# A batch's mixing units over twelve slots instead of ten, with six feed-forward units held back instead of four

## The chip, the cores and the metric

The kernel runs on one core of one Trainium2 chip. The metric is the device time of one execution in microseconds. The engines are named as in the profile: PE (TensorE matmuls), PEld (TensorE weight loads), DVE (VectorE), ACT (ScalarE), POOL (GpSimd) and SP (SyncE, which issues most of the DMAs here).

## What is computed

For 8 batches of 576 positions: causal attention with a decay (8 heads of 64), then a block that mixes along the positions with a rank of 32 and a feed-forward network of width 2048, with a residual. Cut to what matters:

```python
scores = scale * q @ k.T + (cum[:, None] - cum[None, :])      # causal, cum = cumsum(log f)
x = softmax(scores) @ v                                       # heads side by side: (8, 576, 512)
h = x.T @ U @ V                                               # mixing along the positions
u = x + h.T
out = u + relu(u @ w_ch1) @ w_ch2
```

## The kernel before

**Two sweeps.** The first does all of attention, the mixing, and the part of the feed-forward network that belongs to 6 of the 16 blocks of the hidden width. The second, behind it, does the other 10 blocks. The change is in the first.

**Steps and slots.** Attention goes by pairs of heads: 32 pairs, four to a batch. `step(t)` (line 808) is a software pipeline over them: in step t the pair t is scored, the pair t-1 is turned and multiplied with its values, the pair t-2 is finished. Steps 0 to 31 score; 32 and 33 only finish. Each step has 10 slots (`SLOTS`, line 761), which are numbered 0 to 9 here. In every slot PE gets a few short pieces of attention: a score block `S` or `St` (lines 354 to 358), transposes of the exponentials `T` (453, 467), the values `V` in slots 0 and 7 (528, 556), and some more (`Ty`, `Tx`, `Tt`). Behind them a slot can hold a mixing unit and a filler.

**Who follows a score.** DVE takes the row maximum from the score's bank (378, 404), ACT the exponential (386, 414), which frees the bank. Scores have two PSUM banks (`psS`, line 108; up to pair 5 they borrow from `psF` too), so a score waits for the exponential of the score two before it.

**Mixing units.** When the last pair of batch b has been finished (line 907, at the end of slot 9 of the step before `MIX[b]`), `mix_units(b)` gives ten units: five `H` (`hmix`, line 650: one matmul of 128x512, after which DVE adds it to x, line 651), four `Tu` (line 664: four transposes, then ACT copies them to `uh`, line 654, and DVE writes the remainder `ul`, line 655, two slots later) and one `Tv` (line 673). `MIX` is step 6 for batch 0, then 10, 14, up to 30; the last batch's mixing comes after step 33, in a loop of its own (line 954).

**Feed-forward units, the fillers.** `ffn_units(b)` gives 24 units, 27 for odd b: `A` (`l1`, line 713: 12 matmuls of 128x256 or 128x384; ACT takes the relu into `hh`, line 721, and DVE the remainder `hl`, line 717) and `B` (`l2`, line 731: 6 matmuls of 128x512 into an accumulator that three units share, after which DVE adds x and writes `ost`, line 745). They are placed by `credit` (lines 897 to 903) over the slots of `ROOM` (all but 0 and 7), so that `HELD` of them are left when the next batch's mixing starts; those are run in the mixing slots. A batch's own fillers become available when its mixing is over (line 910).

**Banks.** `H`, `Tu`, `Tv`, `A` and `B` share the pool `psF` of two PSUM banks (line 107). While a `B` accumulator is open over its three units, the others have one bank between them.

**Order.** PE's order is as written in `step`. DVE, ACT and POOL are ordered by a scheduler from the order in which `defer` (line 266) hands their work over.

**After step 33** the loop at line 954 interleaves the last batch's mixing and fillers with the loading and splitting of the second sweep's weights (`wb_unit`, line 939), one unit of each to a pass; the splitting runs on DVE and ACT. This stretch is called the drain here.

Of the kernel before, what the change touches and what calls it, by code (L numbers as in the profile page):

```python
# [40 lines left out]
def tile_decay_attention_moe(ctx, tc, qk, v, f, U, V, w1, w2, out):  # L41
# [219 lines left out]
    filler = []  # L261
# [12 lines left out]
    def run_filler():  # L274
        w, fn = filler.pop(0)
        fn()
        return w
# [482 lines left out]
    NP = B * NHP  # L760
    SLOTS = 10
    ENGINES = (nc.scalar, nc.scalar, nc.gpsimd, nc.gpsimd, nc.gpsimd)
    HELD = 4
    with tc.manual_schedule(engines=None):
        fr, fl, cm0, dq = decay_log()
        nc.sync.dma_start(fr, f)
# [39 lines left out]
    MIX = [SEQ.index(NHP * b + NHP - 1) + 3 for b in range(B)]  # L806

    def step(t):
# [3 lines left out]
        last, ending = t == LAST, t > LAST - 2  # L812
# [7 lines left out]
        for s in range(6 + 2 if last else SLOTS):  # L820
# [69 lines left out]
                ranks(c)  # L890

            if mixing:
                for _ in range(2 if t == MIX[0] else 1):
                    mixing.pop(0)[1]()
                if filler and (s in (0, 1, 3, 5) or ending):
                    run_filler()
            elif len(filler) > HELD and s in ROOM:

                ahead = sum(x >= s for x in ROOM) + len(ROOM) * (min(m for m in MIX if m > t) - 1 - t)
                credit[0] += (len(filler) - HELD) / max(ahead, 1)  # L900
                if credit[0] > 0.999 or t > LAST - 3:
                    credit[0] = max(credit[0] - 1, 0)
                    run_filler()
            if ps_ and s == 6:
                score(p, 1, 0)
            if px and s == (6 + 1 if last else 9) and st[c]["hp"] == NHP - 1:
                b = st[c]["b"]
                assert len(filler) <= HELD and not mixing
                mixing.extend(mix_units(b))
# [9 lines left out]
    with tc.manual_schedule(engines={ET.PE, ET.SP}):  # L919
        step(0)  # L920
    with tc.manual_schedule(engines={ET.PE}):
        for t in range(1, 7):
            step(t)
    with tc.manual_schedule(engines={ET.PE, ET.SP}):
        for t in range(7, LAST + 1):
            step(t)
        run_later()
# [584 lines left out]
```

## Time and profile before

| | us |
|---|---|
| three runs | 1223.8, 1224.58, 1919.21 |
| their median | 1224.58 |
| the profiled execution's own time | 1222.74 |
| its span in the trace | 1221.0 |
| step 6, the mixing of batch 0 | 25.01 |
| step 10, the mixing of batch 1 | 20.69 |
| step 30, the mixing of batch 6 | 20.75 |
| start of step 0, of step 6 and of step 32 | 10.7, 95.8, 670.7 |

The third run of the three stands far from the others and is not used. A step's start is that of its first score on PE. A row of a timeline begins with the start and the duration in us; a number in brackets behind it is how long the engine had been idle and for what. Matmul rows overlap, since the array is pipelined: how long one takes is the distance to the start of the next, not its duration. A row of the windows has the stretch, its length, and then each engine's busy time with its instructions in brackets.

### The profile page before, as it was taken

How to read it: one execution, taken by the hardware profiler on the slowest of the kernel's cores; microseconds unless marked ns; L12 is line 12 of the kernel's file. 1: busy time of each engine (PE TensorE's matmuls, PEld its weight loads, DVE VectorE, ACT ScalarE, POOL GpSimd, SP SyncE). 2: the span in 40 equal slices, each digit the busy share in tenths (PEclk: the TensorE clock that was granted, in tenths of full speed). 3: DMA queues.
4: the chain of work that ended last, by engine and by line, in shares of the span. 5: the costliest groups of instructions: out<-in, count | busy, mean ns of one | idle time of the engine just before them, and what ended most of it. 6: DMA issues, size and time to landing. Idle time of an engine off the chain costs nothing.

```text
span 1221.0 us, 23840 instructions
## 1 busy us (share of the span) xinstructions
PE 1187.8 (97%) x8460; PEld 1084.5 (89%) x8460; DVE 930.3 (76%) x2229; ACT 739.1 (61%) x2027; POOL 541.0 (44%) x538
## 2 busy tenths in 40 slices
PE   8998999999999999999999999999999999999998
PEld 5887898988889988989989888788899999999998
DVE  8887878768778778787686798875777767777675
ACT  7777787767768768777676443334454544545443
POOL 4214554444545435454442000125785556555553
PEclk9999999999999999999999999999999999999999
DMA  5753335335235325425232347132514254243420
GB/s 150 198 139 121 102 93 165 97 80 167 80 81 167 95 73 153 116 71 175 80 103 75 121 154 225 42 104 85 140 53 139 87 139 122 90 136 92 134 53 35
DMA packets 81159, 138.47 MB, mean 113 GB/s; under 512 B 8752, under 2 KB 45616, under 8 KB 78992
## 3 DMA queue, kind: packets, MB, share of 16 engines
q1 hardware_dynamic: 79824, 128.56, 34.9%
q0 software_dynamic: 1152, 8.39, 3.8%
q8 instruction: 67, 1.10, 0.4%
q14 instruction: 52, 0.43, 0.1%
q10 hardware_dynamic: 64, 0.00, 0.0%
HBM read 101.08 MB, written 35.78 MB: 112 GB/s over the span
## 4 chain that ended last, share of the span: by engine, by line
PE 78%; DVE 10%; ACT 6%; DMA 3%; issue 2%; SPq 0%; POOL 0%; DVEq 0%; ACTq 0%; POOLq 0%
PE N L1155 12%; PE A L713 10%; PE A L1135 9%; PE B L731 8%; PE B L1135 7%; PE V L556 5%; PE T L453 4%; PE V L528 3%; PE S L357 3%; PE S L358 2%; DMA sr<-in_w_dram 2%; PE B L1155 2%; PE S L354 2%; PE O L1027 2%; PE O L1220 2%
## 5 line engine op out<-in xcount | busy, mean ns | idle before, releaser
L386 ACT ACTIVATE P<-S,nm 128x128 f32<-128x128 f32 (+3 forms) x256 | 137.8, 540 | 53.8 <-DVE nm L378 47.0
L378 DVE CUSTOM_DVE_ANT_0 S<-S,mask 128x128 f32<-128x128 f32 (+3 forms) x256 | 125.6, 496 | 53.4 <-PE S L358 46.7
L197 POOL TENSOR_TENSOR hb<-xn,hb 128x256 fp32r<-128x256 f32 x136 | 114.2, 860 | 117.3 <-ACT hb L194 99.8
L322 POOL CAST G<-qk 64x576 fp32r<-64x576 f32 x52 | 34.8, 669 | 248.7 <-PE St L358 148.0
L713 PE MATMUL A<-uh,w1h 128*128 128x256 f32 (+1 forms) x384 | 120.5, 314 | 1.9 <-DVE hl L717 1.9
L713 PE MATMUL A<-ul,w1h 128*128 128x256 f32 (+1 forms) x384 | 113.5, 296 | 0.0
L713 PE MATMUL A<-uh,w1l 128*128 128x256 f32 (+1 forms) x384 | 113.5, 296 | 0.0
L194 ACT CAST hb<-xn 128x256 fp32r<-128x256 f32 x136 | 51.8, 404 | 76.6 <-DVE xn L1141 42.8
L731 PE MATMUL B<-w2h,hh 128*128 128x512 f32 x216 | 90.4, 418 | 2.0 <-DVE ost L745 1.0
L453 PE MATMUL T<-ident,P 128*128 128x128 f32 x544 | 85.5, 272 | 0.0
L731 PE MATMUL B<-w2l,hh 128*128 128x512 f32 x216 | 85.0, 394 | 0.0
L731 PE MATMUL B<-w2h,hl 128*128 128x512 f32 x216 | 84.6, 391 | 0.0
L435 DVE TENSOR_TENSOR PTl<-T,PTh 128x512 fp32r<-128x512 f32 (+1 forms) x156 | 79.0, 525 | 6.7 <-ACT PTh L432 6.4
L1155 PE MATMUL N<-sw,hb 128*128 128x256 f32 x546 | 80.9, 283 | 1.0 <-POOL hb L197 0.9
L335 POOL TENSOR_TENSOR G<-qk,G 64x576 fp32r<-64x576 f32 x52 | 74.5, 1434 | 13.1 <-ACT G L322 5.1
L1155 PE MATMUL N<-b2h,hb 128*128 128x256 f32 x420 | 79.8, 282 | 0.0
L336 POOL TENSOR_TENSOR G<-qk,G 64x576 fp32r<-64x576 f32 x52 | 75.4, 1449 | 4.8 <-ACT G L322 4.7
L713 PEld LDWEIGHTS A<-uh,w1h 128*128 128x128 f32 x384 | 72.8, 190 | 4.3 <-DVE hl L717 4.1
L357 PE MATMUL S<-G 128*128 128x128 f32 x208 | 70.2, 343 | 4.9 <-ACT P L386 3.1
L432 ACT CAST PTh<-T 128x512 fp32r<-128x512 f32 (+1 forms) x156 | 68.4, 470 | 10.0 <-PE T L453 9.5
L1155 PEld LDWEIGHTS N<-sw,hb 128*128 128x128 f32 x546 | 71.8, 190 | 1.8 <-POOL hb L197 1.8
L713 PEld LDWEIGHTS A<-uh,w1l 128*128 128x128 f32 x384 | 73.1, 190 | 0.3
(327 smaller groups left out, 4012.2 us busy)
## 6 DMA issues: line engine op xcount, KB each, us to landing
qk<-in_qk_dram SPq DMA_DIRECT2D x104, 288.0 KB
direct<-ud SPq DMA_DIRECT2D x48, 256.0 KB
sr<-in_w_dram SPq DMA_DIRECT2D x20, 512.0 KB
vr<-in_v_dram SPq DMA_DIRECT2D x32, 256.0 KB
accd<-ost SPq DMA_DIRECT2D x32, 256.0 KB
xn<-accd SPq DMA_DIRECT2D x8, 1024.0 KB
out_dram<-xn SPq DMA_DIRECT2D x32, 256.0 KB
ud<-uh SPq DMA_DIRECT2D x7, 1024.0 KB
```

Source lines behind the costliest of these rows:

```text
L197: leng.tensor_tensor(dl, src, dh.bitcast(F32), op=ALU.subtract)
L335: pin(el.tensor_tensor(g[oth, 2, cols], k[oth], gf[oth, 2, cols], op=ALU.subtract))
L336: pin(em.tensor_tensor(g[own, 1, cols], q[own], gf[own, 0, cols], op=ALU.subtract))
L357: nc.tensor.matmul(ps, G[j][:, 0, c0 : c0 + P], G[j][:, 2, cols], start=first, stop=False)
L378: newest["top"] = nc.vector.tensor_tensor_reduce(ps[:, :w], ps[:, :w], mask[:, 512 - w : 512], scale=-SCALE, scalar=3.0e38, op0=ALU.add, o ...
L386: nc.scalar.activation(pt, ps[:, :w], AF.Exp, bias=z["nm"][:, col : col + 1], scale=-1.0, accum_out=z["sm"][:, col : col + 1])
L435: defer(2, lambda: nc.vector.tensor_tensor(dstl, src, dsth.bitcast(F32), op=ALU.subtract))
L453: nc.tensor.transpose(tp[:, P * x : P * x + P], z["P"][j][i][:, P * c : P * c + P], ident)
L713: nc.tensor.matmul(ps[:, :nt], wt[:, fc, c], ut[:, c, sl], start=m == 0, stop=m == 3 * NDC - 1)
L731: nc.tensor.matmul(ps, ht[:, fc, P * x : P * x + P], wt[:, fc], start=fc == 0 and m == 0, stop=fc == NA - 1 and m == 2,)
L1135: nc.tensor.matmul(ps, a[x][:, c], b[y][:, c], start=start and m == 0, stop=m == 5, skip_group_check=not start)
L1155: nc.tensor.matmul(ps[:, y], a[p_][:, P * y : P * y + P], w[q_], start=start and y == 0 and m == 0, stop=stop and y == 1 and m == 2,)
```

## The change

Three things, all in `step`:

- `HELD` goes from 4 to 6: two more feed-forward units of a batch are still to be run when the next batch's mixing starts, and so fewer are placed in the slots before.
- In a mixing step of batches 1 to 6, slots 4 and 9 (`SKIP`) take no mixing unit, so the ten units go over slots 0, 1, 2, 3, 5, 6, 7, 8 and, in the next step, 0 and 1. Slots 4 and 9 take a filler instead; with the slots 0, 1, 3 and 5, which had one before, that is six.
- Batch 0, in step 6, gets one mixing unit per slot over slots 0 to 9; before it was two per slot over slots 0 to 4. Its fillers are available from the end of slot 9 instead of slot 4.

```diff
     NP = B * NHP
     SLOTS = 10
     ENGINES = (nc.scalar, nc.scalar, nc.gpsimd, nc.gpsimd, nc.gpsimd)
-    HELD = 4
+    HELD = 6
+    SKIP = (4, 9)
     with tc.manual_schedule(engines=None):
         fr, fl, cm0, dq = decay_log()
         nc.sync.dma_start(fr, f)
...
             if mixing:
-                for _ in range(2 if t == MIX[0] else 1):
+                if t == MIX[0] or s not in SKIP:
                     mixing.pop(0)[1]()
-                if filler and (s in (0, 1, 3, 5) or ending):
+                if filler and (s in (0, 1, 3, 5) or s in SKIP or ending):
                     run_filler()
             elif len(filler) > HELD and s in ROOM:
```

The slots of `ROOM` that hold no filler, in the steps between two mixings (slots 0 and 7 never hold one, and a mixing unit in slots 0 and 1 is not counted):

| step | before | now |
|---|---|---|
| 7 | 4, 9 | 1, 5 |
| 8 | 3, 8 | 1, 6 |
| 9 | 3, 8 | 2, 6 |
| 12, 13 | 2; none | 1; 3 |
| 15, 16, 17 | 6; 3; 1, 5 | 6; 2, 6; 2, 6 |
| 20, 21 | 9; none | 2; 3 |
| 23, 24, 25 | 6; 3, 9; 6 | 6; 2, 6; 2, 6 |
| 28, 29 | 5; none | 2; 3 |

No instruction is added or removed; they stand elsewhere. In the names below the first number is the batch or pair, the last one only tells buffers apart.

PE in step 6, from the first mixing unit of batch 0, before:

```order
L650 MATMUL H0_0_1268<-TS0_624,VV_112 128x512
L650 MATMUL H0_1_1270<-TS0_624,VV_112 128x512
L357 MATMUL S6_01_1284<-G0_91 128x256
L358 MATMUL S6_01_1284<-G0_91 128x256
...
L650 MATMUL H0_2_1291<-TS0_624,VV_112 128x512
L650 MATMUL H0_3_1293<-TS0_624,VV_112 128x512
L357 MATMUL S6_02_1301<-G0_91 128x384
L358 MATMUL S6_02_1301<-G0_91 128x384
```

and now:

```order
L650 MATMUL H0_0_1268<-TS0_624,VV_112 128x512
L357 MATMUL S6_01_1281<-G0_91 128x256
L358 MATMUL S6_01_1281<-G0_91 128x256
...
L650 MATMUL H0_1_1288<-TS0_624,VV_112 128x512
L357 MATMUL S6_02_1295<-G0_91 128x384
L358 MATMUL S6_02_1295<-G0_91 128x384
```

Two units that followed each other are now a slot apart, and the last of the ten stands in slot 9.

PE in step 10, the end of the mixing of batch 1, from its second `Tu`, before:

```order
L664 MATMUL Tu1_1_2542<-ident_99,xn1_105 128x128 x4
...
L664 MATMUL Tu1_2_2579<-ident_99,xn1_105 128x128 x4
L357 MATMUL S10_12_2593<-G1_92 128x384
...
L664 MATMUL Tu1_3_2611<-ident_99,xn1_105 128x128 x4
L357 MATMUL S10_13_2633<-G1_92 128x512
L358 MATMUL S10_13_2633<-G1_92 128x512
L673 MATMUL Tv1_2636<-ident_99,xn1_105 128x64 x4
L357 MATMUL S11_00_2657<-G0_91 128x128
```

and now:

```order
L664 MATMUL Tu1_1_2563<-ident_99,xn1_105 128x128 x4
L357 MATMUL S10_12_2577<-G1_92 128x384
...
L664 MATMUL Tu1_2_2595<-ident_99,xn1_105 128x128 x4
L357 MATMUL S10_13_2617<-G1_92 128x512
L358 MATMUL S10_13_2617<-G1_92 128x512
L731 MATMUL B0_256_1_2472<-w2h_109,hh0_256_2091 128x512
...
L357 MATMUL S11_00_2644<-G0_91 128x128
...
L664 MATMUL Tu1_3_2668<-ident_99,xn1_105 128x128 x4
```

The `B` accumulator `B0_256_1`, which before was closed in slot 5, is now opened in slot 4 and closed in slot 9, with `Tu1_0`, `Tu1_1` and `Tu1_2` in slots 6, 7 and 8 inside that stretch; `Tu1_3` and `Tv1` have moved to slots 0 and 1 of step 11.

DVE at the start of step 11, around the remainder of `Tu1_3`, before:

```order
L378 ISA S10_13_2633,nm10_2353<-S10_13_2633,mask_93 128x512
L378 ISA nm10_2353 128x1
L655 TENSOR_TENSOR ul0_1311<-Tu1_3_2611,uh0_1310 128x4x128
L378 ISA S11_00_2657,nm11_2641<-S11_00_2657,mask_93 128x128
L378 ISA nm11_2641 128x1
L655 TENSOR_TENSOR ul0_1311<-Tv1_2636,uh0_1310 128x4x64
```

and now, from the values of that step:

```order
L576 TENSOR_TENSOR xT9_2550<-V9_1_2647,cr9_1_2648 64x576
L378 ISA S11_01_2681,nm11_2626<-S11_01_2681,mask_93 128x256
L378 ISA nm11_2626 128x1
L435 TENSOR_TENSOR PTl10_2661<-T10_00_2663,PTh10_2660 128x512
L378 ISA S11_02_2700,nm11_2626<-S11_02_2700,mask_93 128x384
L378 ISA nm11_2626 128x1
L655 TENSOR_TENSOR ul0_1351<-Tu1_3_2668,uh0_1350 128x4x128
```

The remainder of `Tu1_3` stood ahead of every score of step 11 on DVE; it now stands behind the values `V9_1` and behind the score `S11_02` of slot 2, the slot in which the batch's first `A` unit stands on PE.

## The prediction

> **What bounds the kernel now.** The page first: PE is busy nearly all the time, the others are not.
>
> ```profile
> span 1221.0 us, 23840 instructions
> PE 1187.8 (97%) x8460; PEld 1084.5 (89%) x8460; DVE 930.3 (76%) x2229; ACT 739.1 (61%) x2027; POOL 541.0 (44%) x538
> ```
>
> All the idle time of PE is 1221.0 - 1187.8 = 33 us. The change adds and removes no instruction, so what it can win or lose is waits of PE. Next the windows, cut at the starts of steps: 6, 7, 8 with 9, 10 and 30, and the drain.
>
> ```profile
> core 0: us, PE busy (x) PEld busy (x) DVE busy (x) ACT busy (x) POOL busy (x), PEclk, DMA share, GB/s
> 95.81:120.82 25.01, 21.76 (x170) 18.70 (x168) 17.54 (x50) 16.88 (x49) 8.86 (x8) 1.00 0.37 122
> 120.82:142.86 22.04, 20.90 (x161) 19.03 (x159) 18.19 (x50) 15.99 (x47) 11.74 (x10) 1.00 0.34 86
> 142.86:180.92 38.06, 37.99 (x280) 35.30 (x278) 29.93 (x90) 31.06 (x90) 21.26 (x19) 1.00 0.36 96
> 180.92:201.61 20.69, 20.02 (x136) 17.19 (x134) 17.97 (x48) 15.74 (x45) 9.98 (x9) 1.00 0.37 101
> 617.06:637.81 20.75, 20.09 (x136) 17.21 (x134) 17.75 (x47) 15.04 (x43) 9.53 (x9) 1.00 0.36 101
> 685.00:770.00 85.00, 79.52 (x401) 66.07 (x400) 79.28 (x163) 33.68 (x66) 1.00 (x1) 1.00 0.51 164
> ```
>
> PE idles 3.25 us in step 6, 1.14 in step 7, 0.07 in steps 8 and 9, 0.66 to 0.67 in a later mixing step, 5.5 in the drain. Third, the waits of PE, which name these:
>
> ```profile
> PE S L357 <- ACT P L386: 3.1, 4, 0.9
> PE Tu L664 <- DVE ost L745: 2.1, 6, 0.3
> ...
> PE H L650 <- DVE xn L651: 1.3, 2, 0.8
> PE B L731 <- DVE ost L745: 1.0, 6, 0.2
> PE Tu L664 <- DVE ul L655: 1.0, 1, 1.0
> PE S L357 <- ACT Ptl L414: 1.0, 4, 0.2
> ...
> PE Tv L673 <- DVE ul L655: 0.7, 1, 0.7
> ```
>
> H, Tu and Tv in step 6 wait 3.0 us for the evacuation of a bank; in the six later mixing steps one Tu and one B each wait for a B's evacuation (3.1 us in all). So the mixing waits that the change is near come to about 6 us, half a per cent. A wait costs more than its idle time, because the array runs empty:
>
> ```profile
> 182.60 0.60 PE L453 MATMUL T<-ident,P 128*128 128x128 f32 x4
> 182.95 0.48 PE L650 MATMUL H<-TS,VV 128*128 128x512 f32 x1
> ...
> 194.67 0.60 PE L453 MATMUL T<-ident,P 128*128 128x128 f32 x4
> 195.62 0.66 PE L664 MATMUL Tu<-ident,xn 128*128 128x128 f32 x4 [0.35 <-DVE ost L745]
> 198.36 0.60 PE L664 MATMUL Tu<-ident,xn 128*128 128x128 f32 x4
> 200.02 0.62 PE L664 MATMUL Tu<-ident,xn 128*128 128x128 f32 x4
> 201.25 0.43 PE L673 MATMUL Tv<-ident,xn 64*128 64x64 f32 x4
> ```
>
> Four transposes take 0.35 us to the next start without a wait and 0.95 with one of 0.35: the wait cost 0.6, its idle time and 0.25 more. I count 0.25 for every wait.
>
> **Part one, the first batch.** In step 6 one unit per slot leaves each evacuation a slot of time, as in step 10, where no H waits. Two A units also leave the step for step 7; that moves work and is no gain. What keeps step 6 from gaining all of its idle time is the next wait in line, that of the scores for their banks:
>
> ```profile
> 110.92 1.25 ACT L322 CAST G<-qk 128x576 fp32r<-128x576 f32 x2
> 112.07 0.64 ACT L432 COPY PTh<-T_v 128x256 f32<-128x256 f32 x2
> 112.60 0.51 ACT L414 ACTIVATE Ptl<-St,nm 128x288 f32<-128x288 f32 x1
> 113.00 0.21 ACT L414 ACTIVATION_READ_ACCUMULATOR Ptl<-St,nm 128x1 f32 x1
> 113.09 0.51 ACT L414 ACTIVATE Ptl<-St,nm 128x288 f32<-128x288 f32 x1
> ```
>
> The casts need the tail scores St done; only after them come the exponentials that free the banks for the scores of slots 6 and 7, 2.7 us later (110.92 to 113.60). An A unit stood over that time:
>
> ```profile
> 189.63 1.37 PE B L731 x6
> ...
> 204.90 1.44 PE A L713 x12
> ```
>
> Without its 1.44 PE has transposes and two Tu, four groups at 0.35 to 0.45, some 1.6 us, and waits about 1.1. Step 6: up to 3.25 gained, about 1.6 given back there and in the scores before. Step 7 is less crowded at its start, since slots 0 and 1 have no filler; I let it gain 0.7 of its 1.14. Together -2.4 us, bounds -4.4 (both steps without idle time) and +1 (the scores wait as long as the units did).
>
> **Part two, slots that are left empty.** Batch 0's fillers now start a step later, and two fewer are placed in each batch, so more slots of ROOM hold none. An empty slot has its price where ACT is behind, as in step 17, whose slot 1 is empty:
>
> ```profile
> 335.87 0.64 ACT L575 COPY cr<-V 64x576 f32<-64x576 f32 x1 [1.15 <-PE V L556]
> 336.29 0.49 PE L453 MATMUL T<-ident,P 128*128 128x128 f32 x3
> 336.41 0.72 ACT L194 CAST VS<-vr 128x640 fp32r<-128x640 f32 x1
> 337.16 0.37 ACT L386 ACTIVATE P<-S,nm 128x128 f32<-128x128 f32 x1
> 337.67 0.44 PE L357 MATMUL S<-G 128*128 128x384 f32 x1 [0.89 <-ACT P L386]
> ```
>
> cr, VS and the exponential stand in a row, and the score of slot 2 waits 0.89, so 1.1 us. An empty slot 6 before the empty 7 costs 0.5 (the four waits for Ptl, 0.25 each, and 0.25) to 0.7; an empty slot 2 or 3 from nothing to 0.4. Step 8 now leaves 1 and 6 empty and step 9 leaves 2 and 6: 1.1 + 0.6 and 0.4 + 0.6, less the 0.3 that steps 8 and 9 lose now: +2.3 (bounds 0 and +3.5). In steps 11 to 29 more slots 2 and 6 go empty, but slots that cost much now (1 of step 17, 5 of step 17, the score of slot 8 in steps 13, 21 and 29) are filled or relieved; I take +0.5, bounds -3 and +3.
>
> **Part three, the six later mixing steps.** Removed: the waits of B, Tu and Tv, 0.67 of idle time and three times 0.25, and the wait of a score behind Tv, about 0.3: 1.7 us a step. Added: with B open from slot 4 to slot 9, Tu in slots 6, 7 and 8 have one bank, so each needs the remainder ul of the one before. The one in slot 7 has the values V behind its predecessor, over 2 us of PE, and need not wait. The one in slot 8 has this before it:
>
> ```profile
> 198.61 0.64 ACT L575 COPY cr<-V 64x576 f32<-64x576 f32 x1 [0.23 <-PE V L556]
> 199.28 0.75 DVE L576 TENSOR_TENSOR xT<-V,cr 64x576 f32<-64x576 f32 x1 [0.49 <-ACT cr L575]
> 199.96 0.55 DVE L378 CUSTOM_DVE_ANT_0 S<-S,mask 128x384 f32<-128x384 f32 x1
> 200.43 0.68 DVE L655 TENSOR_TENSOR ul<-Tu,uh 128x512 fp32r<-128x512 f32 x1
> ```
>
> The chain hangs on the end of V, just ahead of the Tu of slot 7 (198.36), and ul ends at 201.11; in the kernel before Tv takes that bank at 201.25. The Tu of slot 8 comes at 200.02. In the new order it needs that same bank, so it waits until 201.25: 1.2 us. Behind it on PE are the score of slot 9 and the closing B.
>
> The second new wait is that of the batch's first A unit, in slot 2 of the next step. It takes the bank of the last Tu, in slot 0, whose ul stands behind V's chain, a score, a remainder of transposes and the score of slot 2 itself. With
>
> ```profile
> L435 DVE TENSOR_TENSOR PTl<-T,PTh 128x512 fp32r<-128x512 f32 (+1 forms) x156 | 79.0, 525 | 6.7 <-ACT PTh L432 6.4
> ```
>
> that is, from the end of V, cr 0.64, xT 0.75, score 0.5, PTl 0.53, score 0.55, ul 0.68, with about 0.1 between engines: 3.8 us. PE has eight short groups of 0.25 to 0.45 there, some 2.5 us. It waits 1.3 (bounds 0.5 and 1.9). Per step 1.2 + 1.3 - 1.7 = +0.8, times six +4.8; bounds -3 (the second wait absent) and +9.
>
> [...]
>
> **Part four, the drain.** Two B units (2 x 1.37 = 2.7) now run among the last batch's mixing instead of before it. DVE is busy 79.28 of 85.00 us there and PE idles 5.5, so the units fill waits: 2.2 of the 2.7 are covered, I estimate, since the waits lie spread (bounds 0 and 2.7). If DVE were not late there, all 2.7 would be on the path.
>
> **The sum.** -2.4 + 2.3 + 0.5 + 4.8 - 2.2 = +3.0 us on the profiled execution's 1222.74: 1225.7. The two runs at 1223.8 and 1224.58 lie 1.45 above that execution on average, so 1227.2 on their scale. That is +0.2%; 2% is about what a measurement of this kernel can tell from no change.
>
> **The rivals.** (a) *The new waits stay out*: the units in one bank find it free. Then a mixing step gains its 1.7: 6 x (0.8 + 1.7) = 15 below the forecast, 1212. For it: the two B waits do go away, and DVE has less to do in slots 5 and 6. Against it: the chain from V does not depend on a backlog. With one of the two waits it is 1220. (b) *Slower: ACT falls behind in the emptier slots.* If each of the 14 slots 1, 2 and 6 that are newly empty in steps 8 to 29 cost 0.85, between step 17's 1.1 and the 0.6 of a slot 6, they come to 11.9 instead of the 2.8 of part two: +9, 1236. It decides once scores wait in most of those steps. For it: step 17. Against it: slots 7 and 8 of step 9 are empty now, and steps 8 and 9 idle 0.07 us together. (c) *The drain hides nothing*: the two units come where DVE is not late, 2.2 more, 1229. (d) *More slack than PE's busy time shows.* If the time without weight loads were slack that better spread units could use, as the windows have it, 6.3 us in step 6 and 3.5 in each of six steps, that is 27 us: 1197. Against it: steps 8 and 9 lack 2.8 us of loads while PE idles 0.07, so that time is the matmuls' own.
>
> [...] The trace shows 89% against 97% and shows the loads idle where PE is not, so the matmul time is what I count by.
>
> **How the numbers follow.** Forecast 0.55 (1221 to 1233, its own bounds), (a) 0.17, (b) 0.20, (c) 0.06, (d) 0.02. The range 1214 to 1236 leaves out (d), the lower part of (a) and the upper end of (b). More than 2% faster needs (d): 0.02. More than 2% slower needs 25 us, 4 in each mixing step, more than twice my bounds: 0.02. Within 2%: 0.96.
>
> **What would show it.** Right: in the waits of PE, "Tu <- DVE ul" and "A <- DVE ul", some six times each and near 1 us; no "Tu <- DVE ost"; steps 10 and 11 together some 0.8 us longer for the same work; step 6 near 20 us. Wrong: no Tu waits in slot 8 (part three), step 6 below 19 us (part one), or "S <- ACT P" over 10 us (rival b).

## The result, and the profile after

The changed kernel takes 1236.88 us (median of 5 runs, 1236.5 to 1238.91), the kernel before 1223.8 in the same round: 1.0121 times as long, 95% interval 1.0109 to 1.0133 (the ratio is an estimate of its own, not the quotient of the two medians, which is 1.0107). That is 13 us slower and 0.9 us beyond the upper end of the predicted range; the forecast, 1227.2, was on the right side and some 10 us short.

The profiled execution of the changed kernel is 2.0 us above its median. The first lines of its page:

```profile
span 1237.1 us, 23871 instructions
PE 1192.1 (96%) x8460; PEld 1089.3 (88%) x8460; DVE 935.9 (76%) x2229; ACT 739.1 (60%) x2027; POOL 539.6 (44%) x538
```

PE now idles 45 us instead of 33 and is busy 4.3 us longer with the same 8460 instructions. The waits of PE after the change:

```profile
PE A L713 <- DVE ul L655: 8.5, 6, 1.4
PE Tu L664 <- DVE ul L655: 7.1, 12, 0.7
PE S L357 <- ACT P L386: 3.8, 6, 0.9
PE A L713 <- DVE hl L717: 2.8, 4, 1.0
PE S L357 <- ACT Ptl L414: 2.4, 7, 0.5
PE O L1028 <- DVE hb L999: 2.0, 1, 2.0
```

The first line is new, and in the second six of the twelve waits were not expected; "Tu <- DVE ost" and "B <- DVE ost" (3.1 us together) are gone. The windows, cut at the starts of the same steps as before (6, 7, 8 with 9, 10) and over the drain:

```profile
95.72:116.83 21.11, 18.70 (x145) 15.66 (x143) 16.28 (x47) 15.33 (x46) 9.11 (x9) 1.00 0.17 46
116.83:139.70 22.87, 21.27 (x174) 19.91 (x172) 19.40 (x55) 17.98 (x52) 12.55 (x12) 1.00 0.57 175
139.70:180.27 40.57, 39.11 (x280) 35.50 (x279) 30.12 (x88) 30.58 (x89) 20.54 (x19) 1.00 0.34 90
180.27:203.16 22.89, 21.70 (x140) 18.99 (x139) 18.84 (x50) 16.53 (x46) 10.19 (x10) 1.00 0.30 80
698.32:784.00 85.68, 79.96 (x402) 66.85 (x403) 78.94 (x163) 34.79 (x67) 1.00 (x1) 1.00 0.53 169
```

Step 6 still idles 2.4 us, steps 8 and 9 now 1.5 instead of 0.07, a mixing step 1.2 instead of 0.7. Since two B units run later, lengths are compared for the same work in this table (1.37 us for each B unit that a stretch has less or more):

| stretch | before | now | difference | of it work | rest | forecast |
|---|---|---|---|---|---|---|
| steps 6 to 9 | 85.11 | 84.55 | -0.56 | -2.7 | +2.2 | -0.1 |
| steps 10 to 29 | 436.14 | 444.84 | +8.70 | 0 | +8.7 | } +5.3 |
| step 30 to the first T of the last pair | 44.46 | 49.08 | +4.62 | +1.4 | +3.2 | } |
| from there to PE's end | 554.07 | 557.55 | +3.48 | +1.4 | +2.1 | -2.2 |

The rest sums to 16.2 us, within 0.1 the difference of the two spans, where the forecast had 3.0. Each difference is one execution against one. Steps 10 and 11 alone, before and now:

```profile
180.92:223.85 42.93, 42.20 (x305) 38.14 (x304) 34.96 (x99) 34.01 (x96) 21.13 (x19) 1.00 0.50 147
```

```profile
180.27:226.35 46.08, 43.41 (x311) 39.49 (x310) 35.58 (x99) 33.86 (x95) 20.58 (x19) 1.00 0.47 137
```

They take 3.15 us more, 1.37 of it for one B unit more: 1.8 us a mixing step, where the prediction had 0.8. Steps 14 and 15, 18 and 19, 22 and 23, 26 and 27 give the same, 1.75 to 1.78 us each, and all other steps from 10 to 29 together -0.1: the whole of the 8.7 lies in the mixing steps and the steps just behind them. Where it goes shows in the order of time. The transposes of slot 7, which "need not wait" (timeline of the changed kernel, start, length, engine):

```profile
196.50 0.68 DVE L435 TENSOR_TENSOR PTl<-T,PTh 128x512 fp32r<-128x512 f32 x1
...
197.10 0.42 DVE L378 CUSTOM_DVE_ANT_0 S<-S,mask 128x256 f32<-128x256 f32 x1
...
197.44 0.68 DVE L655 TENSOR_TENSOR ul<-Tu,uh 128x512 fp32r<-128x512 f32 x1
...
198.27 0.63 PE L664 MATMUL Tu<-ident,xn 128*128 128x128 f32 x4 [0.46 <-DVE ul L655]
```

The remainder of the Tu before them is queued on VectorE behind a remainder of transposes and a score, and ends at 198.12. Later, the Tu of slot 8 and the first A unit:

```profile
200.84 0.63 PE L664 MATMUL Tu<-ident,xn 128*128 128x128 f32 x4 [0.73 <-DVE ul L655]
...
205.09 0.64 ACT L575 COPY cr<-V 64x576 f32<-64x576 f32 x1 [1.18 <-PE V L556]
205.28 0.60 PE L664 MATMUL Tu<-ident,xn 128*128 128x128 f32 x4
...
205.77 0.75 DVE L576 TENSOR_TENSOR xT<-V,cr 64x576 f32<-64x576 f32 x1 [0.99 <-ACT cr L575]
...
206.44 0.41 DVE L378 CUSTOM_DVE_ANT_0 S<-S,mask 128x256 f32<-128x256 f32 x1
...
207.21 0.60 ACT L654 CAST uh<-Tu 128x512 fp32r<-128x512 f32 x1
...
207.35 0.69 DVE L435 TENSOR_TENSOR PTl<-T,PTh 128x512 fp32r<-128x512 f32 x1 [0.39 <-ACT PTh L432]
...
207.96 0.56 DVE L378 CUSTOM_DVE_ANT_0 S<-S,mask 128x384 f32<-128x384 f32 x1
...
208.43 0.69 DVE L655 TENSOR_TENSOR ul<-Tu,uh 128x512 fp32r<-128x512 f32 x1
...
209.26 0.36 PE L713 MATMUL A<-uh,w1h 128*128 128x256 f32 x1 [1.43 <-DVE ul L655]
```

This is the chain that the prediction had worked out: the fourth Tu is done at 205.88, its ul runs 2.6 us later, behind V's evacuation, two scores and a PTl, and A waits 1.43 us for the bank. In the kernel before, that ul is over well ahead of the first A unit, which doesn't wait:

```profile
202.57 0.69 DVE L655 TENSOR_TENSOR ul<-Tu,uh 128x512 fp32r<-128x512 f32 x1
...
204.66 0.36 PE L713 MATMUL A<-uh,w1h 128*128 128x256 f32 x1
```

One more loss had no place in the sum: the granted clock. In the windows of the changed kernel, 3.41 us wide, before and behind the first A unit of the last pair's step and before and behind the wait of O:

```profile
650.91:654.32 3.41, 1.92 (x15) 1.37 (x14) 2.99 (x8) 3.38 (x12) 1.55 (x1) 1.00 0.22 82
654.32:657.73 3.41, 3.41 (x16) 3.11 (x16) 0.98 (x5) 0.83 (x3) 0.00 (x0) 0.50 1.03 374
...
780.61:784.02 3.41, 1.36 (x6) 0.84 (x5) 3.41 (x9) 1.55 (x4) 0.00 (x0) 1.00 0.18 73
784.02:787.43 3.41, 3.41 (x9) 2.63 (x8) 3.41 (x9) 0.41 (x1) 0.00 (x0) 0.50 0.00 0
```

The number behind those of POOL is the clock: 0.50 for 3.41 us, twice, and PE is busy throughout, so up to 1.7 us are lost each time. In the profile of the kernel before no such stretch lies within the work of PE. That is one execution: the mean clock of its others lies between 0.997 and 1.000, so it need not be free of them.

### The profile page after: what moved, and what is told of

Read it like the earlier page. It is cut to its first block, busy times and chain, and to the rows that moved or that the text cites. A ratio compares the mean times of both kernels' runs of the same rounds, so it can differ in the third digit from the quotient of the medians.

```text
span 1237.1 us, 23871 instructions
## 1 busy us (share of the span) xinstructions
PE 1192.1 (96%) x8460; PEld 1089.3 (88%) x8460; DVE 935.9 (76%) x2229; ACT 739.1 (60%) x2027; POOL 539.6 (44%) x538
## 4 chain that ended last, share of the span: by engine, by line
PE 70%; DVE 9%; ACT 7%; DMA 2%; issue 2%; POOL 0%; DVEq 0%; ACTq 0%; POOLq 0%
PE N L1156 11%; PE A L713 9%; PE A L1136 9%; PE B L731 9%; PE B L1136 7%; PE V L556 5%; PE T L453 3%; PE S L357 2%; DMA sr<-in_w_dram 2%; PE S L358 2%; PE O L1221 2%; PE B L1156 2%; PE O L1028 2%; ACT PTh L432 1%; ACT G L322 1%
```

## The experiments

Each ratio is to the kernel before, timed in the same round.

**The first batch alone.** The kernel before with

```diff
-                for _ in range(2 if t == MIX[0] else 1):
+                for _ in range(1):
```

> The kernel before with the first batch's part alone: one mixing unit per slot over slots 0 to 9 of step 6; no empty slots for the later batches, four fillers held. In the trace of the changed kernel step 6 still stands still for 3.9 us, though its mixing units wait for nothing: the scores of slots 2 and 3 (0.93 and 0.77) and the tail scores now wait for the exponentials. Theory (the wait has only changed its place, and the slots that run empty in steps 7 to 9 cost something too): no gain, the start of step 10 about 2 us later once the same work is counted, the whole 1 to 3 us longer than the kernel before, so 1225 to 1227 where before takes 1223.8. Rival (the first batch's part is sound and all of the loss lies in the later batches): 1 to 3 us shorter, 1221 to 1223.

Measured: 1220.6 us, ratio 0.9986 (0.9977 to 0.9995). The rival was right: this part is sound, and the kernel is the only one of the study that beats the kernel before. It is not for the reason that I had, though. Steps 6 to 9 of this kernel:

```profile
96.65:181.64 84.99, 81.12 (x607) 73.20 (x605) 65.62 (x190) 64.57 (x186) 42.27 (x38) 1.00 0.36 102
271.77:354.10 82.33, 81.05 (x582) 73.59 (x581) 63.77 (x186) 63.76 (x182) 41.15 (x37) 1.00 0.41 115
```

They take 84.99 us where before takes 85.11: the 2.4 us that I counted there did not come, as the theory said. The second row is steps 14 to 17, 82.33 instead of 83.63, because the spacing of the fillers falls on other slots there (slot 1 of step 17 has one now, and the score's wait of 0.89 us is gone), which no theory had. Another 1.8 us lie behind the first T of the last pair, where PE's order is the same in both kernels, so this profile doesn't show that the change made them.

**The other batches alone.** The changed kernel with

```diff
-                if t == MIX[0] or s not in SKIP:
+                for _ in range(2 if t == MIX[0] else s not in SKIP):
                     mixing.pop(0)[1]()
```

> The changed kernel with the first batch's part undone: two mixing units per slot over slots 0 to 4 of step 6 as before, the later batches over twelve slots with six fillers held. Theory (the later batches carry most of the loss): 1233 to 1236 where before takes 1223.8 and the changed kernel 1236.9, with Tu <- DVE ul and A <- DVE ul at the changed kernel's 7.1 and 8.5 us. Rival (the first batch's part is what costs): 1226 to 1229.

Measured: 1238.77 us, 1.0127 (1.0114 to 1.0141), with Tu <- DVE ul 8.3 us in 13 waits and A <- DVE ul 8.5 in 6. The later batches carry the whole loss.

**B closed before the transposes.** The changed kernel with

```diff
-                if filler and (s in (0, 1, 3, 5) or s in SKIP or ending):
+                if filler and (s < 6 or ending):
```

> The changed kernel with the six held fillers in slots 0 to 5 of a mixing step instead of 0, 1, 3, 4, 5 and 9, so that the last B accumulator is opened in slot 3 and closed in slot 5, before the transposes Tu of slots 6, 7 and 8; slots 4 and 9 still take no mixing unit, HELD stays 6. Theory of one bank (Tu waits in slots 7 and 8 because the open B leaves it one bank): the twelve waits Tu <- DVE ul (7.1 us) go, six short waits Tu <- DVE ost of 0.3 come back in slot 6, A <- DVE ul stays near 8.5 us; per mixing step 0.65 + 0.92 - 0.6 = 1.0 less, 5 to 7 us in all, 1230 to 1232 where the changed kernel takes 1236.9. Rival (the remainders ul are late because DVE is behind there, with one bank or two): the waits stay or move to Tv and A, and the time is within 2 us of the changed kernel's.

Measured: 1235.4 us, 1.0101 (1.0085 to 1.0116). Its waits:

```profile
PE S L357 <- ACT P L386: 8.9, 14, 0.9
PE A L713 <- DVE ul L655: 8.5, 6, 1.4
```

The twelve waits Tu <- DVE ul are gone, so the one bank made them. But scores now wait 5.1 us more for the exponentials, above all the first one of the next step (0.8 us in step 11), since slot 9 holds no unit. The gain over the changed kernel is 0.1 to 0.2% and the intervals overlap: the theory had the wait right and its worth, 5 to 7 us, wrong. Part of that is the clock: this profile has two stretches of half clock in steps 19 and 23, where the changed kernel's has none. Where there is none in either, a mixing step with the one behind it is 0.5 us shorter than in the changed kernel (45.5 against 46.1 in steps 10 and 11), some 3 us over six.

**B held open in the kernel before.** The kernel before with

```diff
-                if filler and (s in (0, 1, 3, 5) or ending):
+                if filler and (s in (0, 4, 5, 9) or ending):
```

> The kernel before with one thing changed: its four held fillers stand in slots 0, 4, 5 and 9 of a mixing step instead of 0, 1, 3 and 5, so that the last B accumulator is open from slot 4 to slot 9 over the transposes Tu of slots 5 to 8 and Tv. Ten mixing units over ten slots, four fillers held and the first batch as before. Theory of one bank: the waits Tu <- DVE ost and B <- DVE ost (3.1 us) go, and Tu <- DVE ul comes in slots 6, 7 and 8, Tv <- DVE ul in slot 9, each 0.5 to 1 us: some 3 us added and 1.5 to 2 taken away per mixing step, 6 to 10 us in all, 1230 to 1234 where before takes 1223.8. Rival (the bank waits only take up slack, and the loss of the changed kernel comes from the transposes that moved into the next step and from empty slots): within 2 us of before.

Measured: 1265.5 us, 1.0355 (1.0338 to 1.0371), 43 us over before and more than four times what the theory expected. Waits, and step 10:

```profile
PE Tu L664 <- DVE ul L655: 17.6, 13, 1.7
PE Tv L673 <- DVE ul L655: 10.3, 7, 1.6
PE S L357 <- ACT P L386: 8.3, 10, 0.9
PE B L731 <- DVE xn L651: 5.6, 6, 0.9
```

```profile
181.26:209.75 28.49, 22.12 (x136) 18.40 (x134) 20.55 (x55) 18.34 (x50) 13.12 (x11) 0.94 0.25 66
```

The step takes 28.5 us where before takes 20.7. The transposes of slots 6, 8 and 9 wait 1.7, 1.1 and 1.6 us for the remainder of the one before, that of slot 7, which has V ahead of it, doesn't wait; B waits for H's bank, and the clock is 0.94 over the step. In the changed kernel only the transposes of slots 7 and 8 follow another transpose in the one bank. So the price of one bank depends on how many transposes stand in it and, by the one of slot 7, on what lies between two of them.

**The first A unit a slot later.** The changed kernel with

```diff
-            elif len(filler) > HELD and s in ROOM:
+            elif len(filler) > HELD and s in ROOM and not (s == 2 and t - 1 in MIX[1:]):
```

> The changed kernel with one slot closed to fillers: slot 2 of the step after a mixing step (batches 1 to 6), so that the batch's first A unit stands in slot 3, behind the score of that slot, and the other units move back by one. Theory (the first A unit is early for the remainder ul of the last transposes, and its 1.43 us of idle time also starts stretches in which the granted clock is 0.50): A <- DVE ul falls from 8.5 us to under 2, the stretch of half clock inside the first sweep goes (1.7 us of the changed kernel), and with 0.25 more for each wait the time falls by 8 to 11 us, to 1226 to 1229 where the changed kernel takes 1236.9. Rival (PE is then held by the next one in line, the score of slot 2 or 3 behind the exponentials, or by the units that moved): S <- ACT P grows by 5 us or more and the time stays at 1233 to 1237.

Measured: 1230.32 us, 1.0062 (1.0048 to 1.0076).

```profile
PE S L357 <- ACT P L386: 11.1, 11, 1.1
PE Tu L664 <- DVE ul L655: 7.2, 12, 0.7
```

A <- DVE ul is gone, and the scores wait 7.3 us more, 1.1 in step 11 alone. Both theories are half right: the time fell by some 7 us though the next wait in line took the place of the first. All fillers behind moved too, so this run doesn't say what the A wait is worth.

**Without the late remainder.** The changed kernel, in which GpSimd writes zeros in place of ul for the fourth Tu of batches 1 to 6:

```diff
-            defer(1, lambda: nc.vector.tensor_tensor(dl, src, dh.bitcast(F32), op=ALU.subtract), 2)
+            defer(1, lambda: nc.gpsimd.memset(dl.bitcast(F32), 0.0) if zero else nc.vector.tensor_tensor(dl, src, dh.bitcast(F32), op=ALU.subtract), 2)
```

> The changed kernel without VectorE's remainder ul of the fourth transpose Tu of batches 1 to 6, the one that the batch's first A unit waits for: GpSimd writes zeros into that part of ul instead, so these columns are used without their low part, and the bank of Tu is free once ScalarE has cast uh. Everything else, the matmuls too, is as in the changed kernel. Theory (the bank is held by the late ul alone; uh ends 207.81, when PE is ready for A at 207.83): A <- DVE ul falls from 8.5 us to under 1, its 0.25 each and the stretches of half clock behind it go, and the time is 1226 to 1230 where the changed kernel takes 1236.9. Rival (ScalarE is as late, and the next score takes the wait, as six scores did, S <- ACT P 11.1 us, where the first A unit stood a slot later): S <- ACT P grows by 5 us or more and the time is 1231 to 1236.

Measured: 1229.9 us, 1.0057 (1.0042 to 1.0072).

```profile
PE Tu L664 <- DVE ul L655: 7.2, 12, 0.7
PE S L357 <- ACT P L386: 3.8, 6, 0.9
```

A <- DVE ul does not appear, and S <- ACT P is unchanged. No instruction of PE moved. So ScalarE is not next in line here; six late instructions of VectorE, 0.69 us each, are worth some 0.6% of the kernel, 7 to 8 us. Steps 10 and 11 take 44.72 us instead of 46.08 (182.17 to 226.89 in this profile), and each of the four later pairs of a mixing step and the one behind it is shorter by the same 1.4 us.

**Eleven slots.** The changed kernel with slot 4 alone left out, and fillers in slots 0 to 5 as in the third experiment:

```diff
-    SKIP = (4, 9)
+    SKIP = (4,)
...
-                if filler and (s in (0, 1, 3, 5) or s in SKIP or ending):
+                if filler and (s < 6 or ending):
```

> The changed kernel with slot 4 alone left out of the mixing (slot 9 takes its unit again) and the six held fillers in slots 0 to 5: ten mixing units over eleven slots, so that the fourth transpose Tu stands in slot 9 and only Tv in the next step, and the first A unit in slot 1. The parts tried so far give, over the kernel before: the first batch one to a slot -2 us, HELD 6 alone +1, both with twelve slots +13 to +16. Theory (the price is that of evacuations moved into the first slots of the next step, where ScalarE and VectorE have the values' and the transposes' evacuations as well; Tv is half of one Tu): with Tu back in slot 9 the wait A <- DVE ul goes and a shorter one for Tv's bank or a score takes its place, 3 to 6 us over before, 1226 to 1229. Rival (leaving out any slot costs, since the unit that isn't there leaves PE to wait for the exponentials): half or more of the twelve slots' price stays, 1230 to 1235.

Measured: 1224.34 us, 1.0021 (1.0012 to 1.0030), better than the theory's range.

```profile
PE A L713 <- DVE ul L655: 3.2, 6, 0.5
PE Tu L664 <- DVE ul L655: 2.9, 6, 0.5
```

This kernel and the third experiment's differ in one thing, whether slot 9 has a mixing unit, and so whether the fourth Tu stands there or in slot 0 of the next step, with Tv and the first A unit one slot behind it. That alone is 1.0021 against 1.0101, some 10 us: A's wait is 0.5 instead of 1.4 us, the next step's first score doesn't wait, and the granted clock is 1.00 in steps 18 to 21, where the third experiment's profile has 0.98 with one of its three stretches of half clock; the means of the two executions, 0.996 and 0.995, hardly differ. The pair of runs doesn't part the late transpose from the empty slot 9.

**HELD 6 alone.** The kernel before with

```diff
-    HELD = 4
+    HELD = 6
...
-                if filler and (s in (0, 1, 3, 5) or ending):
+                if filler and (s < 6 or ending):
```

> The kernel before with HELD 6 alone: the six held fillers in slots 0 to 5 of a mixing step, ten mixing units over ten slots, the first batch two to a slot as before. Theory (HELD 6 empties slots of steps 7 to 9 and so on, and costs 2 to 3 us there, as steps 6 to 9 lose 10.9 in the changed kernel against 8.3 where only the first batch's units are spread; the waits Tu <- DVE ul and A <- DVE ul come from the twelve slots and not from HELD): neither of these two waits appears, steps 6 to 9 cost 2 to 3 us more than before for the same work, and the time is 1225 to 1230 where before takes 1223.8. Rival (more held units are harmless, or good, once slots 4 and 9 take their mixing units): 1220 to 1224.

Measured: 1224.21 us, 1.0010 (1.0002 to 1.0019). Steps 6 to 9:

```profile
95.89:179.89 84.00, 78.60 (x594) 71.10 (x593) 65.07 (x189) 64.06 (x184) 41.85 (x37) 1.00 0.36 103
```

84.00 with two B units less is 84.00 + 2.74 - 85.11 = 1.6 us more for the same work. A <- DVE ul does not appear, and Tu <- DVE ul once, in step 6 as before. In these steps the mechanism is the theory's. The total, just below its range, hides two larger parts that no theory had: steps 10 to 29, and the stretch from the first T of the last pair to O's first matmul.

```profile
179.89:611.45 431.56, 425.57 (x2961) 389.83 (x2960) 326.02 (x936) 323.06 (x908) 206.43 (x181) 1.00 0.40 114
658.32:751.86 93.54, 84.91 (x493) 72.73 (x490) 79.45 (x160) 38.56 (x78) 3.32 (x3) 1.00 0.41 138
```

The first is 4.6 us shorter than before (436.14); which of the moved fillers did it was not tried. The second is 4.7 longer than before (88.83) with as many units: two B units that stood ahead of the last transposes Tt now come behind them, and Tt waits 1.19 and 0.75 us where before it doesn't wait.

**Twelve slots with HELD 4.** The changed kernel with

```diff
-    HELD = 6
+    HELD = 4
...
-                if filler and (s in (0, 1, 3, 5) or s in SKIP or ending):
+                if filler and (s in (0, 1, 4, 5) or ending):
```

> The changed kernel with HELD back at 4 everywhere and its four held fillers in slots 0, 1, 4 and 5 of a mixing step, slot 9 empty; the twelve slots and the first batch's spread stay. Theory (the twelve slots carry the loss and HELD little): A <- DVE ul stays at 8 to 9 us, scores wait for the exponentials around the empty slot 9, and the time is 1232 to 1237 where before takes 1223.5 and the changed kernel 1236.9. Rival (it takes the six held units and the twelve slots together): 1223 to 1229.

Measured: 1235.24 us, 1.0101 (1.0088 to 1.0114), A <- DVE ul 8.6 us, S <- ACT P 7.5 in 16 waits. As the theory had it: twelve slots cost about the same with four held units.

**HELD 4 in the last stretch.** The changed kernel with

```diff
-            elif len(filler) > HELD and s in ROOM:
+            elif len(filler) > (4 if t > MIX[-2] else HELD) and s in ROOM:
...
-                credit[0] += (len(filler) - HELD) / max(ahead, 1)
+                credit[0] += (len(filler) - (4 if t > MIX[-2] else HELD)) / max(ahead, 1)
```

> The changed kernel with HELD back at 4 for the last stretch alone, from step 31 on; batches before as in the changed kernel. Theory (the two B units that move into the drain hide nothing there and one of them pushes the decoding of the last weights, whose wait O <- DVE hb grew from 0.7 to 2.0 us with a half clock behind it): 1 to 4 us shorter than the changed kernel, 1233 to 1236, and from the start of the drain's H units to the end as long as before. Rival (the units are covered in the drain as forecast, and the growth there came from elsewhere): within 1 us of the changed kernel's 1236.9 or longer.

Measured: 1238.78 us, 1.0133 (1.0117 to 1.0148). No gain: the time is the rival's. That the units are covered, as the rival says, doesn't follow from it, since the interval overlaps the changed kernel's; nor does the profile settle it, in which the same stretch takes 90.67 us (675.42 to 766.09): the mean clock of this execution, 0.996, comes to an estimated 9.9 us at 0.50 (twice 0.4% of 1236.6), of which the stretches from 300.86 and 655.86 make up 6.8, and the rest can lie there. The drain before O's first matmul, and what follows it, in the changed kernel and in the third experiment's (the same order there):

```profile
674.19:764.23 90.04, 85.56 (x499) 74.17 (x496) 77.21 (x157) 38.63 (x78) 3.31 (x3) 1.00 0.41 140
764.23:1231.74 467.51, 461.53 (x3493) 441.05 (x3491) 338.54 (x604) 208.72 (x552) 243.47 (x257) 1.00 0.35 100
```

```profile
674.41:764.84 90.43, 85.54 (x498) 74.15 (x496) 77.19 (x156) 38.59 (x78) 3.33 (x3) 1.00 0.40 139
764.84:1228.65 463.81, 459.82 (x3493) 439.89 (x3491) 339.09 (x605) 208.68 (x552) 243.56 (x257) 1.00 0.34 100
```

Before has 88.83 and 465.24 for the two. The first stretch is 1.2 and 1.6 longer, with 1.37 of work more by the two orders: next to nothing of it is hidden. The second, 2.3 longer in the changed kernel's profile, is 1.4 shorter in the other with the same order: so the wait O <- DVE hb of 2.0 us and the half clock behind it are more likely that execution's than the change's. (In the second experiment's profile the longest such wait is 1.49, in the kernel before 0.55.)

**Two that tried to win.** The first experiment's kernel with

```diff
-                if filler and (s in (0, 1, 3, 5) or ending):
+                if filler and (s in (0, 2, 3, 4) or ending):
```

> The kernel before with the first batch spread over slots 0 to 9 (the part that by itself took 0.9986 of the time before) and the four held fillers in slots 0, 2, 3 and 4 of a mixing step instead of 0, 1, 3 and 5, so that the last B accumulator is closed one slot before the first Tu and opened one slot later. Theory (the bank waits Tu <- DVE ost 2.1 us and B <- DVE ost 1.0 us are on the path and cost 0.25 more each): both go, 3 to 6 us less than before, 1216 to 1219. Rival (the scores of slots 2 to 4 are pushed and wait for the exponentials, or H takes the wait for the bank): 1220 to 1224.

Measured: 1227.94 us, 1.0046 (1.0033 to 1.0059), worse than either expected.

```profile
PE S L357 <- ACT Ptl L414: 6.0, 12, 0.8
PE B L731 <- DVE xn L651: 4.7, 6, 0.8
```

The waits for ost went, and two others came that were longer: B for H's bank, and the scores behind slot 5, which had lost its cover. And the first experiment's kernel with

```diff
-    HELD = 4
+    HELD = 3
...
-                if filler and (s in (0, 1, 3, 5) or ending):
+                if filler and (s in (1, 3, 5) or ending):
```

> The kernel before with the first batch one to a slot and HELD 3 instead of 4, the three held fillers in slots 1, 3 and 5 of a mixing step (one whole B accumulator, opened in slot 1 and closed in slot 5). Theory (fewer held units fill slots of the steps between that run empty, at 0.3 to 0.8 us each, as six held units cost 1.2 us there; B <- DVE ost goes, since no accumulator closes in slot 0): 1 to 4 us less than the same kernel with HELD 4, which took 0.9986 of the time before: 1217 to 1221 where before takes 1223. Rival (slot 0 of a mixing step needs its filler as cover, as slots 1 and 5 did where the fillers were put earlier): 1222 to 1227.

Measured: 1222.26 us, 0.9997 (0.9988 to 1.0005): the same as before, and no gain over the kernel with four held. H <- DVE xn, 3.0 us in 6 waits, comes in place of B <- DVE ost.

## Why the prediction was wrong

**Part three is the step that failed**, and it failed in its size. It forecast +0.8 us a mixing step; 1.8 was measured in steps 10 and 11 and in each of the four pairs like them, 11.9 for all of steps 10 to 31 where +5.3 stood for parts two and three there. Its two mechanisms are both in the trace, in the places that it named. By the run without the late ul, 1.4 of the 1.8 is the first A unit's wait, which had 1.3; everything else, which had 1.2 added and 1.7 removed, so -0.5, comes to +0.4. What it had wrong:

- *"The one in slot 7 has the values V behind its predecessor ... and need not wait."* It was put at nothing and waits 0.46, six times; with the 0.25 that the prediction adds to a wait that is 0.7 a step. V's matmuls cover PE, but the remainder ul of the predecessor comes two slots later in VectorE's queue and isn't over when V is. I had compared PE's cover with nothing on VectorE's side, though for the Tu of slot 8 and for A I had followed that queue.
- *The Tu of slot 8*, 1.2 in the sum, waits 0.73, or 1.0 with the 0.25. So of the 1.7 that were to be won by the removed waits some 0.4 did not come either; no run shows which.
- *The first A unit* was forecast at 1.3, with bounds, and waits 1.43. Here the chain was right; the run without that ul shows that it alone is 7 to 8 us of the 13.
- *A cost of 0.25 beyond the idle time of each wait* left out the clock. The same 1.43 us wait in the last pair's step was followed by 3.41 us at half clock, up to 1.7 us more than any term of the sum had; with slot 9's unit left out in the third experiment's kernel it happened three times in one execution.

The steps on the way from the kernel before to the changed one, by the ratios of the experiments: the first batch -0.0014; HELD 6 +0.0010; slot 4 left out +0.0025 beyond those two; slot 9 left out +0.0080; a filler in slot 9 instead of slot 2, which holds B open, +0.0020. They sum to 0.0121 by construction: the third is what is left when the first two, which were not run together, are simply added. Each has an interval of 0.001 to 0.002, so the last, and the signs of the small ones, are not sure. The dear step is the one that leaves slot 9 out and puts the fourth Tu into the next step; the late ul, taken out of the changed kernel, makes up 0.0064. The open bank, on which the prediction spent its first term, is small.

One bank for the transposes has the sign of a cost twice: 1.0355 with B held open over all of them; 1.0101 instead of 1.0121 with B closed early, where the intervals overlap. In the changed kernel the larger cost is the queue that frees the bank: 0.0064 for the late ul against 0.0020.

**Part one** forecast -2.4 and, by itself, brought -0.1 in steps 6 to 9: for the same work step 6 gained 1.0 and step 7 nothing, and steps 8 and 9 lost 0.9. The waits of H, Tu and Tv went as it said. It expected the scores to take up 1.1 us in slots 6 and 7; they took up 1.7 (0.93 and 0.77) in slots 2 and 3 already, and A <- DVE hl rose from 0.4 to 1.0 in step 7. The "next wait in line" was named, and given too little.

**Part two** holds: +2.3 forecast for the emptied slots of steps 8 and 9, 2.2 measured for steps 6 to 9 with part one near nothing, 1.6 where HELD alone was changed. Behind them it had +0.5, and the steps between the later mixings came to -0.1.

**Part four** failed: it had 2.2 of 2.7 us hidden in the drain; of the one unit more that runs there, next to nothing is. PE idles 4.83 us before and 4.48 now from the first T of the last pair to O: two waits went (H <- DVE ul 1.28, B <- DVE hl 0.97), and Tt <- DVE xl (0.73), where the B units had stood as cover, and waits of A and B (0.29, 0.53, 0.44) came. That VectorE, busy 79 of 85 us, makes them, since a B unit ends in one more evacuation on it, is likely and was not tried by itself. This is rival (c), which had 0.06. The further 2 us of the profiled drain did not come in the third experiment's profile, which has the same order there.

**Rival (b)** gave nearly the measured time, 1236, for a reason that isn't there: its own sign, "S <- ACT P over 10 us", stands at 3.8. It would have been taken for right by the time alone. Of the prediction's signs, "A <- DVE ul six times near 1 us" and "no Tu <- DVE ost" came true, "step 6 near 20 us" nearly (21.1), and steps 10 and 11 gave the miss. None of its three signs of being wrong came: they were signs that a mechanism is absent, and what failed was a size. It also took 2% as about what a measurement can tell here; the interval of the ratio is 0.12% to either side.

## What to carry to other kernels

When a unit is moved to another slot, follow its evacuation through the queue of the engine that does it: here the bank of a transpose came free 3.2 us after the transpose, 2.6 of them before the last instruction of its evacuation began, and leaving out the last slot of the step, which moves a transpose by one slot into the next, cost some 10 us, where the spread over eleven slots cost 3. Check the cover of every wait on both sides, what PE does meanwhile and what stands ahead on the releasing engine; the wait of the Tu of slot 7, covered on PE's side alone, came six times, 0.46 us each. And an idle stretch of an engine says little about room for more work: in the drain, where PE had idled 4.83 us, next to nothing of one B unit more was hidden, probably because the unit ends on the engine that causes the idle time.

## What the hardware showed that was not expected

TensorE's granted clock was 0.50 in stretches that follow waits of PE. In ten of the fourteen runs the profiled execution has a mean clock of 0.991 to 0.996; it is 0.999 to 1.000 in the kernel before, with the first batch's part alone, with HELD 6 alone and with the fillers in slots 0, 2, 3 and 4. In the profiles of the changed kernel, of the other batches alone, of B closed before the transposes, of B held open, of the later A unit and of HELD 4 in the last stretch, two to four stretches at 0.50 show within the work. All but two are 3.41 us long, those two, with B held open, 6.83, and within a run their starts lie a whole number of 3.41 us apart: 654.32 and 784.02 in the changed kernel are 129.70, that is 38 of them. Where the windows show the 3.41 us ahead, PE was busy in them for 1.1 to 2.1 us, once 2.6, so waits of some 1.3 to 2.3 us, once 0.8, as one or as several, stood there. Not every such wait is followed by half clock: the A wait of 1.43 us comes six times in the changed kernel's profile and is followed by it once, behind the stretch in which PE was busy 1.92 us, that is with 0.06 us more of idle time beside the wait. Some stretches with PE busy as little were not followed by one, in the changed kernel the one from 838.6, with 1.68 us.

The clock also goes with the spread of the times: of the five runs of the changed kernel the shortest, 1236.5 us, has a mean clock of 0.998, the two longest, 1238.28 and 1238.91, have 0.995 and 0.996.
